# Batch 1 and the end in an order written out by hand, and the last value products between gates and in halves

## The chip, the cores and the metric

The kernel runs on one core of a Trainium2 chip. The metric is the device time of one execution in microseconds. Three runs of the kernel before took 674.27, 677.1 and 676.51 us; their median is 676.51.

## What is computed

Eight batches of tokens, 512 local and 32 global ones in each, with 8 heads of 64. Local tokens attend to the global ones and to a window of 32 to each side, global tokens to all; the result is x, with 512 channels. On x stands a feed-forward layer:

```python
x_prev = np.concatenate([np.zeros((B, 1, D)), x[:, :-1, :]], axis=1)
xk = mu_k * x + (1.0 - mu_k) * x_prev
xr = mu_r * x + (1.0 - mu_r) * x_prev
k = np.maximum(xk @ w_k, 0.0)
v = k * k @ w_v
r = 1.0 / (1.0 + np.exp(-(xr @ w_r)))
return (r * v).astype(np.float32)
```

Here w_k is 512x1024, w_v 1024x512 and w_r 512x512, all in f32.

## The kernel before

**Products.** The values are too fine for one pass of TensorE, so each operand is split into a high part (_h) and the rest (_l), and each product is three matmuls: high by high, high by rest, rest by high. The feed-forward layer works on 256 tokens at a time (a *half* of a batch, t0 and t1), the global tokens of all batches are one more set of 256 at the end. A *step* of it is 24 matmuls of 128x128 by 128x256. A half has four steps of keys (K), two of gates (G), and four of values.

**From batch 2 on** (`FROM = 2`) the values k*k @ w_v are made with seven products of blocks in place of eight: the left sides are blocks A11, A21, A12, A22 of w_v and sums S1 to S4 of them, the right sides blocks B11 to B22 of the squared keys and differences T1 to T4. The first three products are `values_1`, the other four `values_2`; `part` makes the two parts of a right side (a cast bh on DVE, the rest bl on DVE or POOL), `left_over` does this for those needed later. The left sides lie in DRAM (`scratch`) and are read back as `a<-scratch`. They are written in batch 1 by `sums_of_values`: for each of four i, two additions on POOL (L279), four more additions and subtractions on POOL (L284 to L287), a cast hs on ACT (L289), the rest ls on DVE (L290), and two stores on SP (L292).

**Mixing** of x with its predecessor (xk, xr) is DVE work with one subtraction on POOL for each of four pieces: k0, k2, r0, r2 (`mixing`, L603 to L613). The older `mix` does all four at once (L572 to L581).

**Attention** of the next pair of heads lies between the steps. For a pair, the steps called A are: four of transposes (four matmuls L144 each into the transpose bank ps_t, then a copy PT on ACT, L408), two of transposes for the global tokens, the second with the next scores, and one of weighted sums. Ahead of the transposes come a softmax on DVE and ACT (L362, L368), its reciprocal sums (L326, L327) and a multiplication on POOL (L374, and L447 for the global tokens).

**What sets the order.** TensorE's order is a chain of dependences in the order in which the program issues its matmuls. For ACT, DVE and POOL a scheduler picks the order, except between `by_hand.enter_context(tc.manual_schedule(...))` and `by_hand.close()`, where instructions stand on their engine in the order in which the code issues them. That stretch is batches 2 to 7. In it `in_turn` takes steps of attention (A) and feed-forward (F) by a string such as "AFAFAFAFAF", and the tables `todo` issue a piece of DVE or POOL work behind a step of a given number. Batch 1 is ordered by the scheduler: `together` spreads A and F evenly and `feed_forward` runs the halves. The end (the global tokens, `end()`) is too, since `by_hand.close()` stands ahead of it.

**PSUM.** ps_t has two banks in batch 1 (`SECOND_USE`) and one in the middle (`MIDDLE_USE`), with three banks ps_m for products; the end has seven of those.

In the text, steps of a batch are numbered from 0: F7 is the eighth feed-forward step, A9 the tenth step of attention.

Of the kernel before, what the change touches and what calls it, by code (L numbers as in the profile page):

```python
# [10 lines left out]
F32 = mybir.dt.float32  # L11
# [9 lines left out]
P = 128  # L21
# [45 lines left out]
def local_global_attention_then_rwkv_ffn(  # L67
# [12 lines left out]
    nc = tc.nc  # L80
# [186 lines left out]
    def sums_of_values():  # L267

        for i in range(HC):
            a = stage.tile([P, 2, 2, TOK], F32, tag="w64", name="a")  # L270
            hs, ls = (stage.tile([P, 4, TOK], F32R, tag="w64", name=f"{x}s") for x in "hl")
            for j in range(2):
                f = i + j * HC
                for x, part in enumerate((wv_h, wv_l)):
                    part = part[:, f].bitcast(F32).rearrange("p (e n) -> p e n", e=2)
                    store = nc.sync.dma_start(out=scratch[:, 2 * j:2 * j + 2, i, x], in_=part)
                    behind(store)
                with tc.issue_after(Tokens.square.ins):
                    nc.gpsimd.tensor_add(  # L279
                        a[:, j], *(w[:, f].bitcast(F32).rearrange("p (e n) -> p e n", e=2) for w in (wv_h, wv_l))  # L280
                    )
            a11, a21, a12, a22 = (a[:, j, e] for j in range(2) for e in range(2))

            nc.gpsimd.tensor_add(a22, a21, a22)  # L284
            nc.gpsimd.tensor_sub(a21, a11, a21)
            nc.gpsimd.tensor_sub(a11, a22, a11)
            nc.gpsimd.tensor_sub(a12, a12, a11)  # L287
            s = a.rearrange("p j e n -> p (j e) n")
            nc.scalar.copy(hs, s)  # L289
            nc.vector.tensor_sub(ls, s, hs.bitcast(F32))  # L290
# [258 lines left out]
    class Tokens:  # L549
# [114 lines left out]
        def values(self):  # L664
            for e0 in range(0, NC, 2):
# [8 lines left out]
                self.store(slice(e0, e0 + 2), o)  # L674
                yield

        def write(self, half, v):

            es = slice(2 * half, 2 * half + 2)
            o = self.gate[:, es]  # L680
            (nc.vector if v.tensor.name.startswith("ps_") else nc.gpsimd).tensor_mul(o, v, o)
            self.store(es, o)

    class Keys:
# [67 lines left out]
                    split(val, h, l, nc.vector if b[0] == "B" else nc.gpsimd)  # L752
                    self.parts[b].append((h, l))

        def product(self, out, b, fresh=True):
            right = self.parts.pop(b)
            for i in range(HC):
                a, (b_h, b_l) = left[i // 2], right[i // 2]
                for j in range(2):
                    a_h, a_l = (a[:, i % 2, x, j * P:(j + 1) * P] for x in range(2))  # L760
                    for n, (w, x) in enumerate(((a_h, b_h), (a_h, b_l), (a_l, b_h))):
                        matmul(
                            out[:, j], w, x[:, i % 2], start=fresh and (i, j, n) == (0, 0, 0),
                            stop=(i, n) == (HC - 1, 2), skip_group_check=True,
                        )
            del left[:HC // 2]
            load_left()

# [47 lines left out]
        def values_of_one(self):  # L816

            t, = self.tokens
            banks = self.bank(), self.bank()
            for b in range(2):  # L820
                parts = self.parts[f"B{b + 1}1"]
                for e, out in enumerate(banks):
                    self.parts[f"B{b + 1}1"] = parts
                    self.product(out, f"B{b + 1}1", fresh=not b)
                    if b:
                        t.write(e, out)
                    yield


    FF_STEPS = 6  # L830
    V_STEPS = 7

    def local_tokens(b, half, xT):
        at = half * TOK
# [11 lines left out]
    def feed_forward(tokens, before):  # L846

        for t in tokens:
            t.mix()
            if before is not None:  # L850
                yield from before.values()
            yield from t.keys_and_gate()
            before = feed_forward.last = t

    PAIR_STEPS = 8

# [187 lines left out]
    beside_heads(rest_of_first(), 2 * FF_STEPS + 2)  # L1044
    line["on"] = True
    leftp = sump = gate3 = None

    def batch(b, before):

        nonlocal leftp, sump, gate3  # L1050
        if b < FROM:
            sums = sums_of_values() if b == FROM - 1 else iter(())
            for n, _ in enumerate(feed_forward(tokens_of(b), before)):
                if n > FF_STEPS and n % 2:
                    next(sums, None)
                yield
            for _ in sums:
                pass
            return
        this = keys_at(b)  # L1060
        t0, t1 = this.tokens
# [15 lines left out]
                t.mixing(x)  # L1077

        def mix_next(*parts):
            if b + 1 < B:  # L1080
                mix(keys_at(b + 1).tokens[0], *parts)

        if b == FROM:
            t0.mix()
            steps = chain(before.values(), this.keys(t0), gates_of(0), this.keys(t1), gates_of(1))
            todo = {
                3: lambda: begin_halves(),
                7: lambda: mix(t1, "k0"),
                8: lambda: (mix(t1, "k2"), this.part("B11", 0)),
# [36 lines left out]
    early_u = valueu  # L1126
    by_hand = ExitStack()
    keys_of = {}

    def keys_at(b):  # L1130
        if b not in keys_of:
# [1 line left out]
        return keys_of[b]  # L1133

    BATCH = {
        FROM: "AFAFAFAFAF" "AFFAF" "AFAFAFAFAF" "AFFAF",
        None: "AFAFAFAFAF" "AFFAFF" "AFAFAFAFAF" "AFFFAFF",
    }
    last = first[1]
    for b in range(1, B):  # L1140
        if b == FROM:
            change_use(MIDDLE_USE)
            line["all"] = True
            by_hand.enter_context(tc.manual_schedule(engines={
                mybir.EngineType.Activation, mybir.EngineType.DVE, mybir.EngineType.Pool,
            }))
        if b < FROM:
            beside_heads(batch(b, last), 2 * FF_STEPS + 8)
            last = feed_forward.last
        elif b < B - 1:  # L1150
# [4 lines left out]
            last = keys_at(b)  # L1155
    final = Keys([global_tokens()])
    t, = final.tokens
    for _ in batch(B - 1, last):
        pass
    last = keys_of[B - 1]  # L1160
    by_hand.close()

    def end():
        t.mix()
# [6 lines left out]
        keys, gates, values = final.keys(t), t.gates(), last.values_2()  # L1171
        n = 5
# [12 lines left out]
    early_u.close()  # L1185


# [45 lines left out]
```

## Time and profile before

| | us |
|---|---|
| median of three runs | 676.51 |
| the profiled execution | 677.94 |
| its span, first to last instruction | 676.2 |
| PE idle between 206 and 216 us, in batch 1 | 5.9 |
| PE idle at the end of values_1 in the end | 2.8 |
| PE idle in the last two products, for a<-scratch | 1.7 |

The profile was taken on another execution than the three runs. Its page lists the busy time of every engine over the span (PE is TensorE's matmuls, PEld its weight loads, DVE VectorE, ACT ScalarE, POOL GpSimd, SP the engine that issues DMAs), the clock that TensorE was granted in 40 slices (9 is full speed), and the chain of work that ended last. Beside the page, the trace gives the waits of an engine with what ended them, the rows of an engine in order of time, and the busy time in any stretch.

### The profile page before, as it was taken

Reading aid. Unit: us, or ns where it says so; the run is one execution under the profiler, and the core shown is the slowest. Engines: PE = TensorE matmul, PEld = TensorE weight load, DVE = VectorE, ACT = ScalarE, POOL = GpSimd, SP = SyncE. Lnnn points to the kernel's source line nnn. Section 1 sums busy time; section 2 is a strip of 40 time slices with the busy share of each in tenths; the row PEclk is TensorE's granted clock in tenths of the full one; section 3 lists DMA queues with packets and bytes.
Section 4 is the critical chain, followed back from the end, with each engine's and each line's share of the span. In section 5 each row is a group of like instructions: output and inputs, shape, how many; then the busy total and the mean of one; then the engine's idle time right before and its main releaser. Section 6 shows DMA issues by size and latency. Waiting matters only on the chain.

```text
span 676.2 us, 20513 instructions
## 1 busy us (share of the span) xinstructions
PE 638.2 (94%) x8362; PEld 605.0 (89%) x8362; DVE 487.4 (72%) x1283; ACT 343.7 (51%) x1070; POOL 358.5 (53%) x326
## 2 busy tenths in 40 slices
PE   6779899999996899999999999999999999999896
PEld 3558789999985899989999999999999999999896
DVE  4687987617468339886989787986898678788531
ACT  4877786537273265737274637364746432313140
POOL 6376776425887124484448453755366435544720
PEclk9789999999998989999999999999999999999899
DMA  8826434514946550645846484727482653282455
GB/s 337 329 95 235 170 127 166 192 46 157 364 139 243 182 191 2 234 157 189 295 180 210 173 272 145 267 109 255 151 295 82 228 179 119 87 291 78 173 181 197
DMA packets 43549, 127.15 MB, mean 188 GB/s; under 512 B 4032, under 2 KB 20928, under 8 KB 43456
## 3 DMA queue, kind: packets, MB, share of 16 engines
q1 hardware_dynamic: 43456, 125.85, 53.0%
q8 instruction: 66, 1.08, 0.6%
q14 instruction: 27, 0.22, 0.1%
HBM read 108.53 MB, written 17.30 MB: 186 GB/s over the span
## 4 chain that ended last, share of the span: by engine, by line
PE 68%; DVE 7%; POOL 5%; ACT 2%; issue 2%; DMA 1%; POOLq 0%; DVEq 0%; ACTq 0%
PE ps_m L141 53%; PE ps_s L141 10%; PE ps_t L144 4%; DVE xfull L576 2%; ACT Pt L368 1%; DVE kkl L629 1%; DMA a<-scratch 1%; POOL Pt L374 1%; POOL a L279 1%; POOL xkl L581 1%; DVE Pt L362 1%; POOL k L625 1%; DVE diff L608 1%; DVE B L715 1%; POOL xrl L581 1%
## 5 line engine op out<-in xcount | busy, mean ns | idle before, releaser
L141 PE MATMUL ps_m<-xkh,wk_h 128*128 128x256 f32 x544 | 156.6, 288 | 4.5 <-DVE sum L785 2.8
L141 PE MATMUL ps_m<-xkh,wk_l 128*128 128x256 f32 x544 | 152.3, 280 | 1.8 <-issue 1.8
L141 PE MATMUL ps_m<-xkl,wk_h 128*128 128x256 f32 x544 | 153.0, 281 | 1.0 <-POOL xkl L581 1.0
L141 PE MATMUL ps_m<-bh,a 128*128 128x256 f32 x736 | 136.6, 282 | 1.7 <-DMA a<-scratch 1.7
L141 PEld LDWEIGHTS ps_m<-bh,a 128*128 128x128 f32 x736 | 114.7, 189 | 2.1 <-DMA a<-scratch 1.5
L374 POOL TENSOR_TENSOR Pt<-Pt,ssum 128x512 f32<-128x512 f32 x64 | 70.8, 1116 | 84.6 <-DVE ssum L327 63.6
L141 PEld LDWEIGHTS ps_m<-xkh,wk_h 128*128 128x128 f32 x544 | 103.7, 191 | 10.1 <-DVE sum L785 3.0
L368 ACT ACTIVATE Pt<-Pt,m 128x128 f32<-128x128 f32 x256 | 99.4, 393 | 14.8 <-DVE m L362 14.3
L141 PEld LDWEIGHTS ps_m<-xkh,wk_l 128*128 128x128 f32 x544 | 104.3, 192 | 2.0 <-issue 2.0
L141 PEld LDWEIGHTS ps_m<-xkl,wk_h 128*128 128x128 f32 x544 | 103.9, 191 | 2.0 <-POOL xkl L581 1.2
L141 PE MATMUL ps_m<-bl,a 128*128 128x256 f32 x368 | 102.7, 279 | 0.2 <-POOL bl L723 0.2
L644 ACT ACTIVATE relu<-ps_m 128x512 f32<-128x512 f32 x52 | 31.0, 596 | 95.2 <-PE ps_m L141 93.6
L141 PE MATMUL ps_m<-xrh,wr_h 128*128 128x256 f32 x272 | 77.1, 283 | 0.5 <-ACT relu L623 0.5
L141 PE MATMUL ps_m<-xrl,wr_h 128*128 128x256 f32 x272 | 75.5, 278 | 0.0
L141 PE MATMUL ps_m<-xrh,wr_l 128*128 128x256 f32 x272 | 75.3, 278 | 0.0
L362 DVE CUSTOM_DVE_ANT_0 Pt<-ps_s,masks 128x128 f32<-128x128 f32 x256 | 56.0, 285 | 20.0 <-PE ps_s L141 20.0
L141 PEld LDWEIGHTS ps_m<-bl,a 128*128 128x128 f32 x368 | 69.2, 188 | 0.4 <-POOL bl L723 0.4
L408 ACT COPY PT<-ps_t 128x512 f32<-128x512 f32 x56 | 32.6, 584 | 67.4 <-PE ps_t L144 67.4
L141 PE MATMUL ps_s<-raw_qk 64*32 64x128 f32 (+1 forms) x2112 | 56.7, 291 | 5.5 <-DMA raw_qk<-qk 5.4
L613 POOL TENSOR_TENSOR xkl<-xfull,xkh 128x512 fp32r<-128x512 f32 x22 | 29.6, 1345 | 57.7 <-DVE ssum L326 34.8
L723 POOL TENSOR_TENSOR bl<-B,bh 128x512 fp32r<-128x512 f32 x36 | 51.2, 1439 | 14.9 <-DVE bh L722 14.9
L722 DVE CAST bh<-B 128x512 fp32r<-128x512 f32 x72 | 49.5, 705 | 10.3 <-PE ps_m L141 10.3
(130 smaller groups left out, 1525.8 us busy)
## 6 DMA issues: line engine op xcount, KB each, us to landing
a<-scratch SPq DMA_DIRECT2D x92, 512.0 KB, 4.8
raw_v<-v SPq DMA_DIRECT2D x32, 896.0 KB, 7.3
raw_qk<-qk SPq DMA_DIRECT2D x32, 624.0 KB, 5.2
out_l<-gate SPq DMA_DIRECT2D x32, 256.0 KB, 4.3
w<-w_k SPq DMA_DIRECT2D x8, 512.0 KB, 9.5
w<-w_v SPq DMA_DIRECT2D x8, 512.0 KB, 3.5
w<-w_r SPq DMA_DIRECT2D x4, 512.0 KB, 3.8
scratch<-wv_h SPq DMA_DIRECT2D x8, 256.0 KB, 6.7
```

The costliest lines, as they stand in the source:

```text
L141: return in_line(nc.tensor.matmul(*a, **kw))
L144: return in_line(nc.tensor.transpose(*a, **kw))
L362: read = nc.vector.tensor_tensor_reduce(out=Pt[:, i], in0=place(t, n, h), in1=masks[:, 2 * slots[t][1] + n], op0=ALU.add, op1=ALU.min, sca ...
L368: nc.scalar.activation(Pt[:, i], Pt[:, i], AF.Exp, bias=low_x[:, i:i + 1], scale=-1.0, accum_out=ssum[:, i:i + 1],)
L374: nc.gpsimd.tensor_mul(Pt[:, some], Pt[:, some], inv.unsqueeze(2).to_broadcast([P, 4, W]))
L408: copy(pitched(j, h, 0, 4), tp.rearrange("p (g q) -> p g q", g=4))
L576: nc.vector.scalar_tensor_tensor(self.shape(xf[:, j]), self.shape(diff[:, j]), mu[:, c0 + j:c0 + j + 1], self.prev(c0 + j), op0=ALU.mult, ...
L581: nc.gpsimd.tensor_sub(lo[:, both], xf, hi[:, both].bitcast(F32))
L613: nc.gpsimd.tensor_sub(lo[:, both], xf, hi[:, both].bitcast(F32))
L644: nc.scalar.activation(rk, kp, AF.Relu)
L722: nc.vector.tensor_copy(h, val)
L723: (nc.vector if b[0] == "B" else nc.gpsimd).tensor_sub(l, val, h.bitcast(F32))
```

## The change

Batch 1 is put under the same regime as the others: the manual schedule and the middle use of the banks begin ahead of batch 1, and it has a string and a table of its own.

```diff
     BATCH = {
+        FROM - 1: "AFAFAFAFAF" "AFFAFFF" "AFAFAFAFAF" "AFFAFFF",
         FROM: "AFAFAFAFAF" "AFFAF" "AFAFAFAFAF" "AFFAF",
...
+    SUMS_AT = range(4, 20)
...
         if b < FROM:
-            sums = sums_of_values() if b == FROM - 1 else iter(())
-            for n, _ in enumerate(feed_forward(tokens_of(b), before)):
-                if n > FF_STEPS and n % 2:
+            t0, t1 = tokens = tokens_of(b)
+            steps = chain(before.values(), t0.keys_and_gate(), t0.values(), t1.keys_and_gate())
+            sums = sums_of_values()
+            todo = {
+                0: lambda: t0.mixing("k2"),
+                1: lambda: t0.mixing("r0"),
+                2: lambda: t0.mixing("r2"),
+                8: lambda: t1.mixing("k0"),
+                9: lambda: t1.mixing("k2"),
+                10: lambda: t1.mixing("r0"),
+                11: lambda: t1.mixing("r2"),
+                18: lambda: keys_at(FROM).tokens[0].mixing("k0"),
+                19: lambda: keys_at(FROM).tokens[0].mixing("k2"),
+            }
+            t0.mixing("k0")
+            for n, _ in enumerate(steps):
+                todo.get(n, lambda: None)()
+                if n in SUMS_AT:
                     next(sums, None)
                 yield
```

The sums of w_v are issued in quarters behind the steps F4 to F19: the first addition, the second, then L283 to L285, then L287 with the cast hs, ls and the stores. Their additions no longer wait for a square of the keys (`issue_after` is gone):

```diff
-                with tc.issue_after(Tokens.square.ins):
-                    nc.gpsimd.tensor_add(
-                        a[:, j], *(w[:, f].bitcast(F32).rearrange("p (e n) -> p e n", e=2) for w in (wv_h, wv_l))
-                    )
+                nc.gpsimd.tensor_add(
+                    a[:, j], *(w[:, f].bitcast(F32).rearrange("p (e n) -> p e n", e=2) for w in (wv_h, wv_l))
+                )
+                yield
...
             nc.gpsimd.tensor_add(a22, a21, a22)
             nc.gpsimd.tensor_sub(a21, a11, a21)
             nc.gpsimd.tensor_sub(a11, a22, a11)
+            yield
             nc.gpsimd.tensor_sub(a12, a12, a11)
             s = a.rearrange("p j e n -> p (j e) n")
             nc.scalar.copy(hs, s)
```

For ACT this gives the following order behind the gates of F8 and F9 in batch 1 (gate_2699), where the four copies PT are those of the transposes A7 to A10 and hs_2737 is the cast of i=1:

```order
L659 ACTIVATE gate_2699<-ps_m_2746 128x512
L661 ACTIVATE gate_2699<-gate_2699 128x1024
L408 COPY PT_206<-ps_t_2793 128x4x128
L408 COPY PT_206<-ps_t_2833 128x4x128
L289 CAST hs_2737<-a_2736 128x1024
L408 COPY PT_206<-ps_t_2874 128x4x128
L408 COPY PT_206<-ps_t_2911 128x4x128
```

Before, the cast of that i stood behind all four copies, and it was the cast of i=0 that stood among them (the gates are the first half's there as well):

```order
L659 ACTIVATE gate_2614<-ps_m_2729 128x512
L408 COPY PT_206<-ps_t_2779 128x4x128
L661 ACTIVATE gate_2614<-gate_2614 128x1024
L289 CAST hs_2598<-a_2597 128x1024
L408 COPY PT_206<-ps_t_2883 128x4x128
L408 COPY PT_206<-ps_t_2914 128x4x128
L408 COPY PT_206<-ps_t_2963 128x4x128
```

A cast stands among the copies in both orders; it is a different i, and the transposes now share one bank. The cast of i=3 stands ahead of the copies of batch 2's first pair in both kernels. On POOL the cast of i=1 stands behind these rows, from the end of i=0 (L374 and L447 are the softmax of the next pair, L613 the mixing of t1, L278 to L287 the sums):

```order
L374 TENSOR_TENSOR Pt<-Pt,ssum 128x512
L613 TENSOR_TENSOR xkl<-xfull,xkh 128x512
L278 TENSOR_TENSOR a<-wv_h,wv_l 128x512
L374 TENSOR_TENSOR Pt<-Pt,ssum 128x512
L613 TENSOR_TENSOR xkl<-xfull,xkh 128x512
L278 TENSOR_TENSOR a<-wv_h,wv_l 128x512
L447 TENSOR_SCALAR Pg<-Pg,ssumg 128x544
L613 TENSOR_TENSOR xrl<-diff,xrh 128x512
L283 TENSOR_TENSOR a<-a 128x256
L284 TENSOR_TENSOR a<-a 128x256
L285 TENSOR_TENSOR a<-a 128x256
L613 TENSOR_TENSOR xrl<-diff,xrh 128x512
```

The next row there is L287, which the cast reads. What moved are the pieces of mixing, which now stand between the additions of one i.

In batch 2 the first half is mixed in pieces: k0 and k2 behind F18 and F19 of batch 1, r0 and r2 behind its own F0 and F1. At the end, the global tokens (`final`) are mixed in batch 7 behind its steps F16 to F18, the last piece behind the first step of the end:

```diff
         def mix_next(*parts):
-            if b + 1 < B:
-                mix(keys_at(b + 1).tokens[0], *parts)
+            mix((keys_at(b + 1) if b + 1 < B else final).tokens[0], *parts)
...
     def end():
-        t.mix()
         for n, _ in enumerate(last.values_1()):
             last.left_over(n)
+            if n == 0:
+                t.mixing("r2")
             yield
```

The order of steps in the end changes as well. Before it was K K V K K V G V G V and then the products of `values_of_one` (E), with the parts of the global tokens' keys by `split` ahead of the E. Now E stands between the gates, and the parts come by `part`:

```diff
-        for stream in (keys, keys, values, keys, keys, values, gates, values, gates, values):
-            next(stream)
-            if stream is values and n < 7:
-                last.left_over(n)
-                n += 1
-            yield
-        for stream in (keys, gates, values):
-            yield from stream
-        final.split("B11", "B21")
-        yield from final.values_of_one()
+        keys, gates, values, ends = final.keys(t), t.gates(), last.values_2(), final.values_of_one()
+        todo = {
+            1: lambda: last.left_over(5),
+            3: lambda: last.left_over(6),
+            4: lambda: final.part("B11", 0),
+            5: lambda: (final.part("B11", 1), final.part("B21", 0)),
+            7: lambda: final.part("B21", 1),
+        }
+        for n, x in enumerate("KVKVKVKVEGEGEE"):
+            next({"K": keys, "V": values, "E": ends, "G": gates}[x], None)
+            todo.get(n, lambda: None)()
+            yield
...
+    by_hand.close()
```

`values_of_one` makes the global tokens' values in two outputs X and Y, each from two products. The last product, of Y, runs its first 128 channels to their end and then the others, each in a bank of its own, so that the first are multiplied by the gate and stored while the others run:

```diff
-        def product(self, out, b, fresh=True):
+        def product(self, out, b, fresh=True, apart=False, between=None):
...
+            steps = [(i, j) for i in range(HC) for j in range(2)]
+            if between:
+                steps.sort(key=lambda x: x[1])
...
+            product(X, 0)
+            yield
+            product(Y, 0, apart=True)
+            yield
+            product(X, 1)
+            t.write(0, X)
+            yield
+            product(Y, 1, apart=True, between=lambda j: t.write_one(2 + j, Y[j]))
+            yield
```

DVE's last rows before (bl are parts of the global tokens' keys, L681 multiplies the gate with a product's 128x512):

```order
L240 TENSOR_TENSOR bl_10109<-B21_9794,bh_10108 128x512
L240 TENSOR_TENSOR bl_10113<-B21_9794,bh_10112 128x512
L812 TENSOR_TENSOR sum_9701<-ps_m_9947,sum_9701 128x512
L681 TENSOR_TENSOR gate_9983<-ps_m_10116,gate_9983 128x512
L681 TENSOR_TENSOR gate_9983<-ps_m_10117,gate_9983 128x512
```

and now (L687 is the former L681, L680 is in `write_one`):

```order
L823 TENSOR_TENSOR sum_9696<-ps_m_9890,sum_9696 128x512
L728 CAST bh_10057<-B21_9793 128x512
L729 TENSOR_TENSOR bl_10058<-B21_9793,bh_10057 128x512
L687 TENSOR_TENSOR gate_10092<-ps_m_10061,gate_10092 128x512
L680 TENSOR_TENSOR gate_10092<-ps_m_10062,gate_10092 128x256
L680 TENSOR_TENSOR gate_10092<-ps_m_10063,gate_10092 128x256
```

The last multiplication is half as large, and a store stands on SP behind each of the two. The number of matmuls is the same in both kernels.

More of the change, by code (lines that the diff above doesn't have):

```diff
@@ L675, in values, with write_one @@
                 yield
+        def write_one(self, e, v):
+            o = self.gate[:, e]
+            nc.vector.tensor_mul(o, v, o)
+            self.store(slice(e, e + 1), self.gate[:, e:e + 1])
         def write(self, half, v):
@@ L753, in split @@
                     self.parts[b].append((h, l))
-        def product(self, out, b, fresh=True):
+        def product(self, out, b, fresh=True, apart=False, between=None):
             right = self.parts.pop(b)
-            for i in range(HC):
+            steps = [(i, j) for i in range(HC) for j in range(2)]
+            if between:
+                steps.sort(key=lambda x: x[1])
+            for i, j in steps:
                 a, (b_h, b_l) = left[i // 2], right[i // 2]
[L759 to L765, printed above, removed]
+                a_h, a_l = (a[:, i % 2, x, j * P:(j + 1) * P] for x in range(2))
+                for n, (w, x) in enumerate(((a_h, b_h), (a_h, b_l), (a_l, b_h))):
+                    matmul(
+                        out[j] if apart else out[:, j], w, x[:, i % 2],
+                        start=fresh and (i, n) == (0, 0) and (apart or j == 0),
+                        stop=(i, n) == (HC - 1, 2), skip_group_check=True,
+                    )
+                if between and i == HC - 1:
+                    between(j)
             del left[:HC // 2]
@@ L818, in values_of_one, with product @@
             t, = self.tokens
[L819 to L826, printed above, removed]
-                    yield
+            X, Y = self.bank(), [self.bank()[:, 0] for _ in range(2)]
+            parts = [self.parts[f"B{b}1"] for b in (1, 2)]
+            def product(out, b, **how):
+                self.parts["end"] = parts[b]
+                self.product(out, "end", fresh=not b, **how)
+            product(X, 0)
[7 more added lines that the diff above has]
+            yield
     FF_STEPS = 6
-    V_STEPS = 7
     def local_tokens(b, half, xT):
@@ L844, in global_tokens @@
                       lambda a: a.rearrange("p (b n) -> p b n", b=GB), store)
-    def feed_forward(tokens, before):
-        for t in tokens:
-            t.mix()
[L850 to L853, printed above, removed]
     PAIR_STEPS = 8
@@ L1058, in batch @@
                 pass
+            batch.last = t1
             return
@@ L1079, in mix_next @@
         def mix_next(*parts):
-            if b + 1 < B:
-                mix(keys_at(b + 1).tokens[0], *parts)
+            mix((keys_at(b + 1) if b + 1 < B else final).tokens[0], *parts)
         if b == FROM:
-            t0.mix()
             steps = chain(before.values(), this.keys(t0), gates_of(0), this.keys(t1), gates_of(1))
             todo = {
+                0: lambda: mix(t0, "r0"),
+                1: lambda: mix(t0, "r2"),
                 3: lambda: begin_halves(),
@@ L1128, in local_global_attention_then_rwkv_ffn @@
     keys_of = {}
+    final = Keys([global_tokens()])
     def keys_at(b):
@@ L1139, in local_global_attention_then_rwkv_ffn @@
     last = first[1]
-    for b in range(1, B):
[L1141 to L1150, printed above, removed]
+    change_use(MIDDLE_USE)
+    line["all"] = True
+    by_hand.enter_context(tc.manual_schedule(engines={
+        mybir.EngineType.Activation, mybir.EngineType.DVE, mybir.EngineType.Pool,
+    }))
+    for b in range(1, B):
+        if b < B - 1:
             ff = batch(b, last)
@@ L1154, in local_global_attention_then_rwkv_ffn @@
                 pass
-            last = keys_at(b)
-    final = Keys([global_tokens()])
+            last = keys_at(b) if b >= FROM else batch.last
     t, = final.tokens
```

4 lines of the change are left out of this document (removed).

## The prediction

> **What bounds the kernel now.** I read the page first, then PE's waits, then its windows.
>
> ```profile
> PE 638.2 (94%) x8362; PEld 605.0 (89%) x8362; DVE 487.4 (72%) x1283; ACT 343.7 (51%) x1070; POOL 358.5 (53%) x326
> ...
> PEclk9789999999998989999999999999999999999899
> ...
> PE 68%; DVE 7%; POOL 5%; ACT 2%; issue 2%; DMA 1%; POOLq 0%; DVEq 0%; ACTq 0%
> ```
>
> PE is busy for 94% of the span, no other engine for more than 72%, and PE carries 68% of the chain that ended last. The change leaves the number of matmuls as it is, so it can only move what PE loses: idle time, and time at a lower granted clock. PE's waits say where the large pieces are:
>
> ```profile
> PE ps_t L144 <- POOL xrl L581: 5.9, 1, 5.9
> ...
> PE ps_m L141 <- DVE sum L785: 2.8, 1, 2.8
> PE ps_m L141 <- issue: 1.8, 1, 1.8
> PE ps_m L141 <- DMA a<-scratch: 1.7, 2, 1.3
> ...
> PE ps_m L141 <- POOL bl L723: 0.2, 1, 0.2
> ```
>
> Columns: total us, times, longest. The windows (length, then busy time and count of PE, PEld, DVE, ACT, POOL, then PEclk) place them:
>
> ```profile
> 130.00:140.00 10.00, 10.00 (x88) 10.00 (x87) 3.69 (x11) 2.07 (x5) 3.50 (x3) 1.00 0.66 262
> ...
> 170.00:180.00 10.00, 9.38 (x81) 9.15 (x81) 7.62 (x11) 2.61 (x4) 8.57 (x8) 1.00 1.03 373
> ...
> 200.00:210.00 10.00, 7.62 (x78) 6.86 (x74) 7.96 (x13) 4.93 (x21) 9.29 (x9) 1.00 1.01 390
> 210.00:220.00 10.00, 5.23 (x25) 5.26 (x26) 9.02 (x15) 3.56 (x5) 5.79 (x5) 0.67 0.33 115
> ...
> 214.77:220.10 5.33, 5.33 (x25) 5.33 (x26) 5.12 (x9) 1.40 (x2) 1.52 (x2) 0.50 0.54 190
> ...
> 237.40:240.60 3.20, 3.20 (x17) 3.20 (x17) 0.00 (x0) 2.73 (x10) 0.00 (x0) 0.50 0.01 5
> ...
> 300.00:620.00 320.00, 320.00 (x4180) 311.66 (x4179) 263.02 (x637) 157.37 (x480) 164.12 (x127) 1.00 0.54 187
> ...
> 629.81:633.20 3.39, 3.39 (x16) 3.39 (x17) 3.39 (x4) 0.00 (x0) 3.39 (x4) 0.51 0.20 82
> ```
>
> From 300 to 620 us PE is busy all the time at full clock: there is nothing to win in the batches that were already ordered by hand. What batch 1 loses is in three rows: 0.62 us in 170 to 180, and 2.38 + 4.77 = 7.15 us in 200 to 220. After that idle time PE runs for 5.33 us at a clock of 0.50, which costs half of it, 2.65. **Batch 1 loses 10.4 us.** The matmul at 130 to 140 gives the unit for what follows: 10.00 us / 88 = 0.114 us each, so 2.73 us for one step of 24. After the end's wait of 2.8 us the clock is 0.51 for 3.39 us: 1.7 lost.
>
> The waits row names xrl, which is one row too late. ACT and POOL at that place:
>
> ```profile
> 212.60 1.04 ACT L289 CAST hs<-a 128x1024 fp32r<-128x1024 f32 x1 [5.86 <-POOL a L287]
> ...
> 214.04 0.58 ACT L408 COPY PT<-ps_t 128x512 f32<-128x512 f32 x1
> ...
> 211.67 0.90 POOL L287 TENSOR_TENSOR a<-a 128x256 f32<-128x256 f32 x1
> ```
>
> PE's next transposes need the only transpose bank, which the copy at 214.04 frees. That copy stands on ACT behind the cast hs, and the cast waited 5.86 us for POOL's last subtraction L287. **The mechanism of the stall is the hs cast ahead of the PT copies in ACT's queue.** So the question for the change is where it puts that cast.
>
> **The change in batch 1.** The 10.4 us go if the new order has no such place. The order has two. The cast of i=1 stands between the copies of the transposes A8 and A9, and that of i=3 ahead of batch 2's first copy. The price is worked out from POOL's durations:
>
> ```profile
> L374 POOL TENSOR_TENSOR Pt<-Pt,ssum 128x512 f32<-128x512 f32 x14 | 16.1, 1169 | 15.5 <-DVE ssum L327 14.1 <-ACT relu L623 1.5
> L625 POOL TENSOR_TENSOR k<-relu 128x512 f32<-128x512 f32 x10 | 11.1, 1112 | 13.3 <-ACT relu L623 13.1
> L279 POOL TENSOR_TENSOR a<-wv_h,wv_l 128x512 f32<-128x512 f32 x8 | 10.9, 1388 | 1.4 <-DVE ls L290 1.4
> ...
> L447 POOL TENSOR_SCALAR Pg<-Pg,ssumg 128x544 f32<-128x544 f32 x4 | 4.0, 1001 | 5.0 <-DVE ssumg L327 5.0
> L286 POOL TENSOR_TENSOR a<-a 128x256 f32<-128x256 f32 x4 | 3.5, 884 | 0.3
> L285 POOL TENSOR_TENSOR a<-a 128x256 f32<-128x256 f32 x4 | 3.3, 815 | 0.2
> L287 POOL TENSOR_TENSOR a<-a 128x256 f32<-128x256 f32 x4 | 3.1, 777 | 0.2
> L284 POOL TENSOR_TENSOR a<-a 128x256 f32<-128x256 f32 x4 | 3.0, 752 | 0.2
> ...
> L613 POOL TENSOR_TENSOR xkl<-xfull,xkh 128x512 fp32r<-128x512 f32 x14 | 18.1, 1291 | 29.1 <-DVE ssum L326 29.1
> L613 POOL TENSOR_TENSOR xrl<-diff,xrh 128x512 fp32r<-128x512 f32 x13 | 17.7, 1359 | 25.2 <-PE ps_t L144 14.2 <-DVE xrh L612 9.4 <-DMA a<-scratch 1.6
> ...
> L368 ACT ACTIVATE Pt<-Pt,m 128x128 f32<-128x128 f32 x256 | 99.4, 393 | 14.8 <-DVE m L362 14.3
> ```
>
> and from batch 2, which has the same softmax and mixing in by-hand order, but no sums of weights:
>
> ```profile
> 249.39 0.60 ACT L644 ACTIVATE relu<-ps_m 128x512 f32<-128x512 f32 x1 [1.18 <-PE ps_m L141]
> ...
> 253.96 1.41 POOL L613 TENSOR_TENSOR xkl<-xfull,xkh 128x512 fp32r<-128x512 f32 x1 [1.61 <-DVE xkh L612]
> ...
> 262.23 1.66 POOL L613 TENSOR_TENSOR xrl<-diff,xrh 128x512 fp32r<-128x512 f32 x1 [0.36 <-DVE xrh L612]
> ```
>
> *First stall.* Count from the start of the relu of step F7. PE needs the copy of A9 when it comes to A10. Ahead of that stand F8 to F12, five steps of 24, and three sets of four transposes: 132 matmuls x 0.114 = 15.0 us. On the other side: relu 0.6, L625 1.1, L287 0.8, the hs cast of i=0 1.0, four L368 of 0.39, and about 0.3 for DVE's reciprocal sums, 5.4. Then POOL does, in its queue's order, two L374 (2.34), two xkl (2.58), two weight additions (2.78), L447 (1.0), two xrl (2.72), L283 to L285 (2.45) and L287 (0.78): 14.65. One wait for an xkh as at 253.96 adds 1.6. L287 ends at 21.65, the cast at 22.7, the copy at 23.3: **a stall of 8.3 us**. From below: batch 2's last xrl ends 14.5 us after its relu began (263.89 - 249.39); were all added POOL work to fit in the idle time of that stretch, then L287, the cast and the copy would still end at 16.9, a stall of 1.9. From above: the slower xkl and xrl beside a busy DVE and two more waits for xrh of a microsecond each, 10.8. I take 8.3, since POOL's rows leave it little idle time there once the sums are in.
>
> *Second stall.* Count from F17's relu. PE reaches A1 of batch 2 after F18, F19, four transposes and F0: 76 x 0.114 = 8.6. POOL: relu 0.6, then L625, one addition, L374, xkl, L283 to L285, L374, xkl, L287: 1.11 + 1.39 + 1.17 + 1.29 + 2.45 + 1.17 + 1.29 + 0.78 = 10.65. With one wait of 1.6, 12.9; cast and copy to 14.5: **5.9 us**, between 4.3 (no wait) and 8 (a second wait, longer operations).
>
> *Clock.* PE's idle time cost 1.6 to 2.65 us more in the rows with 0.50; I take 2.1 for each of the two stalls. Batch 1 then loses 8.3 + 5.9 + 4.2 = 18.4 in place of 10.4: **+8.0**, between -1.0 (1.9 + 4.3 + 2 x 1.6 = 9.4) and +13.7 (10.8 + 8 + 2 x 2.65 = 24.1).
>
> The rest of that part I cost at nothing. Mixing in four pieces is the same DVE and POOL work, in steps in which the values of earlier tokens keep PE fed. The middle banks (one transpose bank, three m) are what batches 2 to 6 have, and those show no idle PE. The hs and ls stores on SP now stand ahead of loads for heads that come a whole pair later; if that cover fails, it shows as a wait for raw_qk or raw_v. The issue gap of 1.8 us, and the 1.6 of clock behind it (the row at 237.40), come in batch 2 behind work that stays; I leave both in.
>
> **The change at the end.**
>
> ```profile
> 619.71 0.41 DVE L572 TENSOR_TENSOR diff<-xg_all 128x256 f32<-128x256 f32 x1
> ...
> 625.58 2.91 DVE L576 SCALAR_TENSOR_TENSOR xfull<-diff,mu_r_sb,xg_all 128x256 f32<-128x256 f32 x2
> ...
> 629.08 0.68 DVE L785 TENSOR_TENSOR sum<-ps_m,sum 128x512 f32<-128x512 f32 x1
> ...
> 667.81 0.69 DVE L681 TENSOR_TENSOR gate<-ps_m,gate 128x512 f32<-128x512 f32 x1 [8.11 <-PE ps_m L141]
> ...
> 669.03 0.39 PE L141 MATMUL ps_m<-bh,a 128*128 128x256 f32 x1 [1.26 <-DMA a<-scratch]
> ...
> a<-scratch SPq DMA_DIRECT2D x92, 512.0 KB, 4.8
> ```
>
> The sum L785, for which PE waits 2.8 us, stands on DVE behind the mixing of the global tokens (2.91 us of L576 alone just before it). With that mixing in batch 7's last steps, where PE's windows show it fed and DVE is 82% busy (263.02 of 320), the wait goes: -2.8, and its clock, -1.7. What is late next: the parts of T3. Before, two steps K stand between the halves and they came just in time (the bl row: 0.2 us of wait). Now one K stands there, so they are due 2.7 us sooner; from above the new wait is 2.9. DVE and POOL have less to do there by the mixing, so it can be nothing. I take 1.2. The last two products waited 1.7 for a<-scratch; now a gate step stands between each, 2.7 us more against 4.8 us from issue to landing, and the slot is free two products earlier: -1.7 (nothing, if the slot isn't). The last multiplication is 128x256 in place of 128x512: 0.41 for 0.69 by the row at 619.71, and half as much to store: together -0.5, an estimate. **The end: -2.8 - 1.7 - 1.7 - 0.5 + 1.2 = -5.5**, between -6.7 (no new wait) and -2.1 (2.9 of wait and 1.7 of clock).
>
> [...]
>
> **Sum.** +8.0 - 5.5 = +2.5 us on the profiled execution's own 677.94 (the span of 676.2 and 1.7 around it): 680.4. That execution lies 1.4 above the median of the three, 676.51; from the median the forecast is 679.0. About 0.5% (3.4 us) is what a measurement of this kernel can tell from no change: faster is below 673.1, slower above 679.9.
>
> **Rivals.**
> - *POOL has the room* (0.22). The sums fall into POOL's idle time, and the stalls come out at 1.9 and 4.3. For it: batch 2's stretch has idle POOL time ahead of three of its operations. Against it: the queue is in order, and the additions stand between operations that wait. -1.0 - 5.5 = -6.5: 670.0.
> - *The hs cast costs all that it can* (0.20), the slower side. ACT's queue holds the copy of A9 behind the cast until POOL's L287 is done. It decides as soon as L287 ends later than 13.4 us after F7's relu (15.0 less cast and copy); at 10.8 and 8 us +13.7 - 5.5 = +8.2: 684.7. For it: the old stall had this very chain.
> - *The end's wait only changes its name* (0.10): PE waits for T3's parts for 2.9 us and loses the clock again. +8.0 - 2.1 = +5.9: 682.4. Against it: less work on DVE there.
> - *The issue gap doesn't recur* (0.13): nothing in the profile names its cause, and a shift of some instructions may remove it: 679.0 - 1.8 - 1.6 = 675.6.
> - The forecast itself (0.35), spread over 676 to 682.
>
> Faster: the first rival and a little of the fourth, 0.23. Slower: the second, the third, and some of the forecast's upper part, 0.37. The rest, 0.40. The range reaches from just above the first rival's value to the second's, 670.5 to 684.5. Both signs hold much of the chance; the forecast's own range is 676 to 682.
>
> **What would show it.** Right: in batch 1 PE waits at L144 of 6 to 10 us with ACT's hs at its end, idle behind POOL a L287; another of 4 to 8 us at batch 2's second transposes; a PEclk of 0.5 behind each; no wait for the sum of L785's place (L796 now), none for a<-scratch in the last products, a short one for bl. Wrong: PE without idle time between 160 and 230 us, then the first sum falls; or PE waits in the end as long as before under another name; or PE waits for raw_qk or raw_v behind the stores on SP.

## The result and the profile after

| | median us | runs | ratio to before |
|---|---|---|---|
| before | 676.01 | 674.27 to 677.1 (4) | |
| changed | 687.18 | 684.15 to 687.46 (4) | 1.0158 (1.0121 to 1.0194) |
| before, other chip | 676.56 | 671.06 to 682.58 (17) | |
| changed, other chip (E6) | 683.83 | 678.19 to 689.63 (6) | 1.0101 (1.0035 to 1.0166) |

The change made the kernel slower, by 1.2 to 1.9% in the first measurement and by 0.4 to 1.7% in the second. The forecast was 679.0 with a range to 684.5: the first median lies outside it, that of the later measurement just inside, and both lie well above the forecast. The profiled execution took 687.01 us, its span is 685.2.

The page of the changed kernel, its busy row, the granted clock in 40 slices and the chain that ended last:

```profile
PE 643.4 (94%) x8362; PEld 609.8 (89%) x8362; DVE 502.7 (73%) x1296; ACT 342.6 (50%) x1066; POOL 354.0 (52%) x326
...
PEclk9977979999889899999999999999999999999999
...
PE 79%; DVE 8%; DMA 4%; POOL 3%; issue 3%; ACT 2%; SPq 0%; POOLq 0%; DVEq 0%
```

PE is as busy as before, 94%. The clock row has its low digits in the first six slices (100 us), as before but lower, and around 190 and 230 us. PE's waits (total us, times, longest):

```profile
PE ps_t L144 <- ACT PT L408: 17.5, 4, 9.5
...
PE ps_m L141 <- POOL bl L729: 2.1, 2, 1.3
...
PE ps_m L141 <- issue: 1.3, 1, 1.3
```

The wait for L785's sum and the waits for a<-scratch are gone. In place of one stall of 5.9 us there are two, of 9.5 and 7.2, and now the view names their releaser rightly: the copy PT on ACT. The first of them, row by row on ACT, POOL and PE (start, length, and in brackets the idle time ahead):

```profile
167.10 0.60 ACT L623 ACTIVATE relu<-ps_m 128x512 f32<-128x512 f32 x1 [1.17 <-PE ps_m L141]
...
190.01 1.05 ACT L289 CAST hs<-a 128x1024 fp32r<-128x1024 f32 x1 [13.17 <-POOL a L287]
190.96 0.58 ACT L408 COPY PT<-ps_t 128x512 f32<-128x512 f32 x1
...
172.30 1.07 POOL L374 TENSOR_TENSOR Pt<-Pt,ssum 128x512 f32<-128x512 f32 x1 [2.78 <-DVE ssum L327]
175.11 1.29 POOL L613 TENSOR_TENSOR xkl<-xfull,xkh 128x512 fp32r<-128x512 f32 x1 [1.75 <-DVE ssum L326]
...
180.22 1.29 POOL L613 TENSOR_TENSOR xkl<-xfull,xkh 128x512 fp32r<-128x512 f32 x1 [1.22 <-DVE ssumg L326]
...
184.22 1.27 POOL L613 TENSOR_TENSOR xrl<-diff,xrh 128x512 fp32r<-128x512 f32 x1 [0.43 <-DVE xrh L612]
...
189.25 0.72 POOL L287 TENSOR_TENSOR a<-a 128x256 f32<-128x256 f32 x1
...
191.68 1.09 PE L144 MATMUL ps_t<-ident,Pt 128*128 128x128 f32 x4 [9.46 <-ACT PT L408]
```

ACT does nothing for 13.17 us and holds a finished set of transposes behind the cast. The releaser to read is that of the cast, POOL's L287. The second stall has the same form:

```profile
214.95 0.60 ACT L623 ACTIVATE relu<-ps_m 128x512 f32<-128x512 f32 x1 [0.70 <-PE ps_m L141]
...
229.19 1.05 ACT L289 CAST hs<-a 128x1024 fp32r<-128x1024 f32 x1 [7.10 <-POOL a L287]
...
230.86 1.09 PE L144 MATMUL ps_t<-ident,Pt 128*128 128x128 f32 x4 [7.24 <-ACT PT L408]
```

Where the time went, from windows of 1 us: idle is the sum of what PE was not busy, clock the sum of its busy time times (1 - PEclk), in us; the last part of a microsecond is left out. E6, E9 and E11 are second and third profiles of the two kernels.

| | 0 to 100 | 100 to 310 | 310 to 600 | from 600 |
|---|---|---|---|---|
| before: idle, clock | 17.3, 6.3 | 11.9, 4.4 | 0.0, 0.0 | 8.6, 1.6 |
| before again (E9) | 16.3, 8.2 | 12.2, 4.0 | 1.1, 0.0 | 7.0, 1.7 |
| changed | 15.7, 15.3 | 20.3, 3.6 | 0.3, 0.0 | 5.3, 0.0 |
| changed again (E6) | 16.5, 9.2 | 21.3, 5.3 | 0.0, 0.0 | 5.0, 0.0 |
| changed again (E11) | 15.7, 11.8 | 20.7, 5.8 | 0.9, 0.0 | 5.4, 0.0 |

By the means of the rows the change costs 25.7 - 16.3 = 9.4 us between 100 and 310 us and gains 9.4 - 5.2 = 4.2 in the end. The third part, 28.1 - 24.1 = 4.0 us more in the first 100 us, lies in a stretch in which both programs have the same instructions in the same order on every engine.

These sums come to 9.2 us, but the profiled executions differ by 6.9 by their means, so they count more than the time that was lost. A count by matmuls adds up. PE's first 1734 matmuls are the same, in the same order, in every profile of the study, and so are its 2703rd to 8026th. Cut at the end of the 1734th and at the starts of the 3501st and the 7851st, the spans fall into these parts, in us:

| | first 1734 matmuls | to the 3501st | to the 7851st | to the end |
|---|---|---|---|---|
| before | 132.3 | 140.5 | 333.6 | 69.8 |
| before again (E9) | 134.0 | 140.3 | 335.4 | 68.7 |
| changed | 138.9 | 147.4 | 334.3 | 64.5 |
| changed again (E6) | 133.5 | 150.0 | 333.8 | 64.8 |
| changed again (E11) | 136.0 | 149.9 | 334.7 | 64.5 |

By the means the change costs 8.7 us in the second part, gains 0.2 in the third and 4.6 in the last, 3.9 in all behind the 1734th matmul. The first part, ahead of the changed code, is 3.0 us longer, and 6.6 in the first pair of profiles.

### The profile page after: what moved, and what is told of

It is laid out like the page before. It is cut to its first block, busy times and chain, and to the rows that moved or that the text cites. A ratio compares the mean times of both kernels' runs of the same rounds, so it can differ in the third digit from the quotient of the medians.

```text
span 685.2 us, 20545 instructions
## 1 busy us (share of the span) xinstructions
PE 643.4 (94%) x8362; PEld 609.8 (89%) x8362; DVE 502.7 (73%) x1296; ACT 342.6 (50%) x1066; POOL 354.0 (52%) x326
## 4 chain that ended last, share of the span: by engine, by line
PE 79%; DVE 8%; DMA 4%; POOL 3%; issue 3%; ACT 2%; SPq 0%; POOLq 0%; DVEq 0%
PE ps_m L141 59%; PE ps_s L141 14%; PE ps_t L144 5%; DMA w<-w_k 2%; DMA raw_v<-v 2%; DVE diff L608 2%; PE ps_t L141 1%; DVE xfull L608 1%; DVE diff L603 1%; DVE B L721 1%; DVE xkh L612 1%; DVE kkl L629 1%; DMA w<-w_r 0%; ACT Pt L368 0%; ACT hs L289 0%
## 5 line engine op out<-in xcount | busy, mean ns | idle before, releaser
L374 POOL TENSOR_TENSOR Pt<-Pt,ssum 128x512 f32<-128x512 f32 x64 | 69.9, 1099 | 87.1 <-DVE ssum L327 51.2
L368 ACT ACTIVATE Pt<-Pt,m 128x128 f32<-128x128 f32 x256 | 99.4, 392 | 13.6 <-DVE m L362 12.9
L613 POOL TENSOR_TENSOR xkl<-xfull,xkh 128x512 fp32r<-128x512 f32 x30 | 40.1, 1336 | 68.2 <-DVE ssum L326 38.5
L362 DVE CUSTOM_DVE_ANT_0 Pt<-ps_s,masks 128x128 f32<-128x128 f32 x256 | 55.9, 285 | 21.8 <-PE ps_s L141 21.5
L613 POOL TENSOR_TENSOR xrl<-diff,xrh 128x512 fp32r<-128x512 f32 x30 | 41.0, 1366 | 46.5 <-DVE xrh L612 28.1
L141 PE MATMUL ps_s<-raw_qk 64*32 64x128 f32 (+1 forms) x2112 | 58.3, 294 | 5.6 <-DMA raw_qk<-qk 5.5
L144 PE MATMUL ps_t<-ident,Pt 128*128 128x128 f32 x256 | 40.4, 285 | 21.5 <-ACT PT L408 17.5
```

The source lines that it names most:

```text
L141: return in_line(nc.tensor.matmul(*a, **kw))
L144: return in_line(nc.tensor.transpose(*a, **kw))
L362: read = nc.vector.tensor_tensor_reduce(out=Pt[:, i], in0=place(t, n, h), in1=masks[:, 2 * slots[t][1] + n], op0=ALU.add, op1=ALU.min, sca ...
L368: nc.scalar.activation(Pt[:, i], Pt[:, i], AF.Exp, bias=low_x[:, i:i + 1], scale=-1.0, accum_out=ssum[:, i:i + 1],)
L374: nc.gpsimd.tensor_mul(Pt[:, some], Pt[:, some], inv.unsqueeze(2).to_broadcast([P, 4, W]))
L613: nc.gpsimd.tensor_sub(lo[:, both], xf, hi[:, both].bitcast(F32))
```

## The experiments

**E1, the end alone.** The diff without its part on batch 1: batch 1 stays with the scheduler, and the global tokens' mixing, the order of steps, `part` and the halves are as changed.

```diff
-        FROM - 1: "AFAFAFAFAF" "AFFAFFF" "AFAFAFAFAF" "AFFAFFF",
...
+        if b == FROM:
+            change_use(MIDDLE_USE)
...
+        if b < FROM:
+            beside_heads(batch(b, last), 2 * FF_STEPS + 8)
+            last = feed_forward.last
```

> The end of the change alone; batch 1 is as before. My theory (the end gains what its waits lost: PE idle 5.3 against 8.6 us and no half clock, so 4.9 us by the two traces): about 671 us, 4 to 6 below before, with a wait of about 2 us for the parts of T3. Rival (the wait only changes its name once batch 1 does not arrive late): no gain, within 2 us of before. On the first 100 us, whose code is the same in all kernels: if the 9 us more of half clock that the changed kernel shows there is chance, this run shows some value between 6 and 15 us; if it belongs to the change in batch 1, it shows about 6 as before.

Measured: 670.77 us (10 runs), ratio 0.9939 (0.99 to 0.9979), beside a kernel before at 675.04. PE's waits in the end:

```profile
PE ps_m L141 <- POOL bl L729: 0.4, 1, 0.4
PE ps_m L141 <- DVE sum L801: 0.3, 1, 0.3
...
PE ps_m L141 <- DVE sum L796: 0.2, 1, 0.2
```

L796 is the former L785: its wait falls from 2.8 to 0.2 us with the mixing moved out of the way. The gain of 4.3 us is what my theory gave. The half clock of the first 100 us came to 3.1 us, less than in any other profile and below what either reading had expected.

**E2, batch 1 alone.** The diff without its part on the end.

```diff
-            mix((keys_at(b + 1) if b + 1 < B else final).tokens[0], *parts)
+            if b + 1 < B:
+                mix(keys_at(b + 1).tokens[0], *parts)
...
     last = keys_of[B - 1]
+    by_hand.close()
...
     def end():
+        t.mix()
```

> Batch 1 by hand alone; the end is as before. My theory (two stalls behind the hs casts, 9.5 and 7.2 us, in place of one of 5.9): PE loses 7.6 us more between 100 and 310 us, so 683 to 684 us if the first 100 us cost the same as before. Rival (the longer half clock of the first 100 us comes with this part of the change): 690 us or more, with 15 us of half clock before 100 us again.

Measured: 683.97 us (4 runs), ratio 1.0111 (1.0042 to 1.018), with 8.9 us of half clock before 100 us. The two stalls are there. What I had not forecast is the rest of its list:

```profile
PE ps_t L144 <- ACT PT L408: 17.5, 4, 9.5
...
PE ps_m L141 <- DMA a<-scratch: 0.2, 1, 0.2
```

The wait for L785's sum isn't there, although the end and its mixing are as before. The static order tells why. The first matmul of the end's first K, before the change and in E2, with the semaphore that it waits for:

```
4849 L141 MATMUL ps_m_9795<-xkh_9642,wk_h_217 128x256 [waits DVE_49]
4846 L141 MATMUL ps_m_9797<-xkh_9644,wk_h_217 128x256 [waits Activation_49]
```

It writes another bank. The banks ps2 are used in turn; batch 1 with the middle use takes another number of them, so the end starts on the bank that ACT's copy L780 frees, early, and not on that of DVE's L785. From the 7851st matmul to the end E2 takes 65.5 us, with the old code there, where the changed kernel takes 64.5 to 64.8 and the kernel before 68.7 to 69.8.

**E3, the casts later.** The changed kernel with hs, ls and their stores apart from L287, a step or more later (i=1 behind F14, i=3 behind F2 of batch 2).

```diff
             nc.gpsimd.tensor_sub(a12, a12, a11)
+            yield
             s = a.rearrange("p j e n -> p (j e) n")
...
-    SUMS_AT = range(4, 20)
+    SUMS_AT = {**dict.fromkeys((4, 5, 6, 7, 9, 10, 11, 15, 16, 17), 1), **dict.fromkeys((8, 14, 18, 19), 2)}
...
+                2: lambda: next(batch.sums),
```

> The changed kernel, but each hs cast with its ls and stores is issued a step or more after L287 (for i=1 behind F14, for i=3 behind F2 of batch 2), so that no copy PT that PE needs soon stands behind it; POOL does the same rows in nearly the same order. My theory (ACT's queue holds the copies): the waits of 9.5 and 7.2 us go to under 1.5 us each, with their half clock of 3 us: 15 to 18 us below the changed kernel, 669 to 672. Rival (POOL is too full there, and PE waits for the next thing that POOL makes late): PE waits at least 4 us in each place under another name, 680 or more.

Measured: 665.99 us (4 runs), ratio 0.9849 (0.9789 to 0.9909), below the 669 to 672 that I had expected. The stall of 9.5 us is gone altogether, that of 7.2 has become 4.2:

```profile
PE ps_t L144 <- ACT PT L409: 5.1, 3, 4.2
...
215.99 1.04 ACT L290 CAST hs<-a 128x1024 fp32r<-128x1024 f32 x1 [7.91 <-POOL a L287]
```

POOL does the same rows in nearly the same order, and PE doesn't wait for it under another name. So it is ACT's queue, not POOL's load. What is left, above the 1.5 us that I had expected, is again a cast ahead of a copy; that i=3 was not put late enough is tried in E7 and E10.

**E4, the cast on DVE.** Same place in the program, other queue.

```diff
-            nc.scalar.copy(hs, s)
+            nc.vector.tensor_copy(hs, s)
```

> The changed kernel, but the hs cast is done by DVE in the same place of the program, so it stands directly ahead of ls in DVE's queue and ACT's queue is free of it. My theory (the wait is for the queue that holds the cast): the copies PT are no longer late, but DVE's rows behind the cast are held until L287 ends, so PE waits 0 to 4 us at scores or at a ps_m bank in each place: 672 to 680. Rival (POOL's fullness alone): as in the changed kernel, 685 or more.

Measured: 666.34 us (4 runs), ratio 0.985 (0.9795 to 0.9905), better than I had expected. The waits:

```profile
PE ps_t L144 <- POOL Pg L447: 3.3, 2, 2.2
...
PE ps_s L141 <- DVE m L362: 1.4, 1, 1.4
PE ps_t L144 <- ACT PT L408: 0.8, 2, 0.6
```

The copies are no longer late. In each place a small wait is left, of 1.4 and 2.2 us. The longer one is for a row that now stands behind the cast in DVE's queue, the sums for L447:

```profile
222.44 0.69 DVE L289 CAST hs<-a 128x1024 fp32r<-128x1024 f32 x1 [2.09 <-POOL a L287]
...
224.32 0.15 DVE L326 TENSOR_SCALAR ssumg<-ssumg 128x1 f32<-128x1 f32 x1
...
224.83 1.11 POOL L447 TENSOR_SCALAR Pg<-Pg,ssumg 128x544 f32<-128x544 f32 x1 [2.42 <-DVE ssumg L327]
```

The wait of 1.4 us goes a longer way: POOL's next addition waited 2.13 us for DVE's ls behind the cast, POOL's L625 stood behind that addition, DVE waited 3.12 us for L625, and the scores' row L362 stood behind that. One changed word takes 16.7 us of waiting down to 3.6: what stands behind the cast in DVE's queue was needed later than what stood behind it in ACT's.

**E5, the banks of the end.** The kernel before with one edit:

```diff
-    LAST_USE = {"m": [ps2, ps2, psx, ps4, ps4, ps4, ps4]}
+    LAST_USE = {"m": [psx, ps2, ps2, ps4, ps4, ps4, ps4]}
```

> The kernel before with one edit: the end's list of banks begins with psx in place of ps2, so that its first step K writes the bank that ACT L780 frees, not the one that DVE L785 frees; the mixing of the global tokens stays where it was. Theory A (what makes PE wait for 2.8 us is which bank the first K gets, as the run of batch 1 alone suggests, where that wait was gone with the end unchanged): no wait for L785's sum, no half clock behind it, 3 to 5 us below before, 670 to 672 us. Theory B (my prediction's reading, that it is the mixing ahead of L785 on DVE): the wait moves to the next K or stays, total PE wait there above 2 us, time within 1.5 us of before.

Measured: 674.67 us (12 runs) beside 676.56, ratio 0.9971 (0.9935 to 1.0008). In the list of waits the sum L785 is gone, with no half clock behind it; a<-scratch is left:

```profile
PE ps_t L144 <- POOL xrl L581: 5.9, 1, 5.9
...
PE ps_m L141 <- DMA a<-scratch: 1.0, 3, 0.5
```

The trace bears theory A out: another bank is enough, with the mixing where it was. The median is only 1.9 us below, where 3 to 5 were expected, and the time does not settle the size, since the interval reaches from 4.4 us faster to no gain. Its one profile does: from the 7851st matmul to the end it takes 64.6 us, 4.6 less than the kernel before by its mean and as little as the changed kernel.

**E6, E9 and E11, both kernels again.** The changed kernel (E6, E11) and the one before (E9), with no edit.

> The changed kernel once more, unchanged, for the clock in the first 100 us. Theory C (the half clock there is chance and has nothing to do with the change; from 100 us on the change costs 3 us): the median comes out 2 to 7 us above before, 678 to 683, with some of its runs at a mean clock of 0.975 or more. Theory D (the changed kernel runs that stretch at half clock for longer as a rule): 686 to 688 again, every run at a clock of 0.970 or less.

> The kernel before once more, for a second profile of it. If the wait of 2.8 us for L785's sum is a matter of banks and order alone, it is there again, between 2.5 and 3.1 us, and the stall of 5.9 us in batch 1 too. If the half clock of the first 100 us is chance, its sum lies anywhere from 3 to 15 us and need not be the 6.3 of the first profile.

> The changed kernel a third time, for its profile: both stalls again, 9.5 and 7.2 us within 0.3, since they follow from the queues; the half clock in the first 100 us is a new draw (15.3 and about 9 us so far). If it is over 12 us here as well, the changed kernel draws high as a rule and chance alone becomes a poor reading.

E6 measured 683.83 us (6 runs), E9 one execution of 680.14, E11 one of 686.89. The stalls and the wait come back within 0.2 us: 9.4 and 9.5 us in the changed kernel, 5.9 and 2.6 in the one before. The rows of E6 and of E9:

```profile
PE ps_t L144 <- ACT PT L408: 17.5, 4, 9.4
...
PE ps_t L144 <- POOL xrl L581: 5.9, 1, 5.9
PE ps_m L141 <- DVE sum L785: 2.6, 1, 2.6
```

The first 100 us do not come back; the row of their window (PE busy and PEclk are the first and the sixth figure behind the length), for the kernel before, the changed one, and the two again in E9 and E11:

```profile
0.00:100.00 100.00, 82.67 (x1269) 66.54 (x1269) 77.09 (x261) 72.47 (x241) 64.62 (x94) 0.93 0.59 213
...
0.00:100.00 100.00, 84.29 (x1129) 67.84 (x1130) 72.06 (x233) 66.64 (x215) 60.88 (x91) 0.85 0.56 203
...
0.00:100.00 100.00, 83.67 (x1237) 67.35 (x1237) 76.97 (x258) 70.87 (x234) 63.12 (x93) 0.91 0.57 208
...
0.00:100.00 100.00, 84.34 (x1156) 68.05 (x1158) 74.92 (x249) 69.24 (x227) 61.78 (x92) 0.88 0.57 208
```

PE's busy time differs by less than 2 us, the clock by up to 0.08, which is 8 us; where the clock is lower, fewer of the matmuls fall into the window. The executions of one kernel follow their mean clock: in E6 from 678.19 us at 0.980 to 689.63 at 0.965. Theory D as it was put (every run at 0.970 or less) falls, since two of the six runs have 0.980. Theory C's 678 to 683 was a little low. That the start is chance alone isn't shown: E11's half clock in the first 100 us, 11.8 us, is just under the 12 above which its expectation called chance a poor reading, and what the other runs add stands under "What stays open" below.

**E7 and E10, the cast of i=3 a step later still.**

```diff
-                2: lambda: next(batch.sums),
-                3: lambda: begin_halves(),
+                3: lambda: (next(batch.sums), begin_halves()),
```

> The casts later, as before, and that of i=3 one step later still (behind F3 of batch 2, ahead of the first load of the left sides). In the first version PE waited 4.2 us for the copy behind that cast, with 1.7 us of half clock. By the queue theory a step more (2.7 us) leaves at most 1.5 us of wait, and 3 to 5 us come off: 661 to 664. If POOL's L287 is itself what is late, the wait moves on with the cast and the time stays at 666.

> The kernel with the casts later and that of i=3 behind F3, once more, since the profile of its first run fell on an execution that was disturbed. By the queue theory PE's wait for the copy behind that cast (4.2 us in the first version) is under 1.5 us, the wait for bl is 2.0 as in the changed kernel, and the time is 661 to 667.

E7's profiled run took 3508 us and is left out; why is not known. The other five took 663.12 to 668.2 us, with a median of 663.44, ratio 0.9855 (0.9802 to 0.9907). E10, the same kernel on another chip, took 660.89 us (4 runs) beside 675.1, ratio 0.9782 (0.9702 to 0.9862). Its waits, and its row for 100 to 310 us:

```profile
PE ps_m L141 <- POOL bl L730: 2.1, 2, 1.3
...
PE ps_t L144 <- ACT PT L409: 0.8, 2, 0.6
...
100.00:310.00 210.00, 206.06 (x2974) 197.45 (x2972) 149.80 (x430) 121.31 (x400) 117.53 (x102) 1.00 0.53 187
```

The wait for the copy is 0.8 us, as in the kernel before, and between 100 and 310 us PE is idle for 4.0 us and never at half clock. The queue's reading holds here too: the wait did not move on with the cast.

**E8, two steps K ahead of the first product.** E7 with:

```diff
-        for n, x in enumerate("KVKVKVKVEGEGEE"):
+        for n, x in enumerate("KKVKVKVVEGEGEE"):
```

The pieces that `todo` issues from `left_over` and `part` come a step later with it.

> As the kernel with the casts two steps later, and the end begins with two steps K ahead of the first product of values_2, as before the change, in place of one. If the wait of 2.0 us for the parts bl is the price of the one K that was taken from between, as the prediction had it, it falls under 0.5 us and the time by 1 to 2 us. If another resource sets it (DVE's queue of parts), the wait comes back at a later product and the time stays.

Measured: 660.73 us (6 runs) beside 676.56 on the same chip, ratio 0.9768 (0.9705 to 0.9831); E7's five runs there have a median of 663.44. The wait for bl:

```profile
PE ps_m L141 <- POOL bl L730: 0.4, 1, 0.4
```

The 1.7 us come off the wait as expected, and from the 7851st matmul to the end the profile takes 62.9 us, 1.7 less than E10's 64.5. The medians of E8 and E7 differ by 2.7 us, but their runs overlap (654.5 to 664.84 and 663.12 to 668.2), so the time alone doesn't show the gain. E8 is the fastest version of the study, some 2.3% below the kernel before, and it holds the whole of the change but for the place of the sums' casts and of one K.

## Why the prediction was wrong

1. *The mechanism of the stalls: right.* The page named xrl; the prediction read the hs cast ahead of the copies. For the changed kernel's two stalls E3 and E4 show it, by moving the cast in time and to another queue. For the old stall no run moved the cast alone, and it rests on the rows that the prediction shows.
2. *The first stall: right in place, too small.* PE's due time was 15.0 us after F7's relu; in the trace it is 191.68 - 9.46 - 167.10 = 15.1. POOL was to begin at 5.4 (172.30 - 167.10 = 5.2). L287 was to end at 21.65 and ended at 22.9 (189.97 - 167.10): POOL waited three times for DVE, for 1.75, 1.22 and 0.43, where the sum took one wait of 1.6. So 9.5 in place of 8.3: POOL's waits for DVE were the term that was too small.
3. *The second stall: the same fault.* 7.2 in place of 5.9; due at 8.7 (8.6 in the sum), L287 at 14.2 (12.9). Together the two are 2.5 us short. Both fell inside the bounds of 10.8 and 8.
4. *The clock behind the stalls: right.* 4.2 was taken; the two windows behind them give 3.12 x 0.43 + 4.94 x 0.45 = 3.6:

```profile
191.68:194.80 3.12, 3.12 (x17) 3.12 (x18) 0.63 (x1) 0.59 (x1) 2.41 (x2) 0.57 0.95 336
230.86:235.80 4.94, 4.94 (x25) 4.94 (x26) 2.32 (x6) 0.59 (x1) 2.38 (x2) 0.55 0.62 216
```

5. *Batch 1 as a whole*: +8.0 in the sum, 8.7 by the count of matmuls and 9.4 by the windows. The wait "issue" of batch 2 came back (1.3 to 2.2 us), as the forecast had it.
6. *The end*: -5.5 in the sum, -4.6 by the count of matmuls and -4.2 by the windows. The new wait for bl was 2.1, not 1.2; E8 shows that it is the price of the K that was taken from between. The waits for a<-scratch did go, but in the second profile of the kernel before they were only 0.6 in place of 1.7, so 1.7 was one execution's value. The smaller last product and store gained 0.8 and not 0.5: from the start of the last matmul to the end of the span it is 4.3 us in both profiles of the kernel before and 3.5 in the three of the changed one.
7. *Why the 2.8 us went: half the reason.* With batch 1 as it was, moving the mixing does it (E1). But the first part of the change does it by itself, through the banks (E2, E5). I looked at what DVE had in its queue and not at which bank PE was about to write. That the term came out near its forecast is luck in this part. The gains of the two parts don't add: E2 with the old end took 683.97 us and the whole change 683.83, each in its own session, and behind the 7851st matmul E2's end is longer by only 0.8 us. Most of what the end part would have won was won already.
8. *The step that failed most: the time ahead of the changed code was put at nothing.* The sum put +2.5 on one execution's own time, as if the rest cost the same in every execution and in both kernels, and the range was built of the stalls' bounds alone. Behind the 1734th matmul the change costs 3.9 us (5.2 by the windows), which puts the forecast at about 680 to 682, inside the range. Of the 9.0 us between the first two profiled spans, 6.6 lie in the first 1734 matmuls. What is longer there is the time at half clock: in the first 100 us it costs 6.3 and 8.2 us in the two profiles of the kernel before, 15.3, 9.2 and 11.8 in the three of the changed one, 3.1 to 14.6 in the other kernels of the study, and the twelve profiles take 128.4 us (at 3.1) to 138.9 (at 15.3) for those matmuls. Three runs between 674.27 and 677.1 looked like a spread of 3 us; the later 17 went from 671.06 to 682.58.

The side was one that the prediction held open, slower with 0.37. The rival that came nearest, the hs cast at its full price, did so in the number alone: its stalls of 10.8 and 8 us did not come, and the start made up the difference.

What stays open: why the changed kernel is slower in its start, and whether it is so as a rule. Its three values can be three high draws, but the other runs lean the other way. An estimate: take from each run's lost clock, (1 - mean clock) x span, what the profiles of its kernel lose behind the 1734th matmul (0.1 to 10.2 us). On average 10.2 us are left in the 38 runs of kernels with batch 1 by hand, and 6.6 in the 60 of kernels with batch 1 by the scheduler; single runs of either kind spread by about 4. From 78 to 96 us PEclk is 0.72 to 0.91 in five of the eight profiles of the first kind and 1.00 in all four of the second. So the change may have a price ahead of its own code, of about 3 us. No run changed the start by itself, and nothing here shows how code that comes later would do it.

## What to carry to other kernels

- In an order by hand, look at each instruction that waits for another engine's last step (here a cast) and ask what stands behind it in its own queue and when that is needed; issue the producer early and the consumer two or three steps later, or put the consumer in a queue whose next rows have time. Here the 16.7 us of waiting came down to 4.2 in E3 and to 3.6 in E4.
- A wait for a bank can depend on the rotation: that of 2.8 us for L785's sum went with a change far ahead that takes another number of banks (E2), and with another first bank alone (E5). So read which bank the waiting instruction writes before giving the wait to the work ahead of its releaser.
- Ask how far the parts of the program that are not touched vary from one execution to the next, and put that in the range: here the same 1734 matmuls took 128.4 to 138.9 us. A median of three runs close together says little of it.
- Compare two profiles from one matmul to the same matmul, where the order allows it, and not only between two times: the parts then add up to the spans.

## What was not expected of the hardware

The clock that PE is granted in the start does not repeat from one execution to the next. In the stretch whose instructions are the same, from 44 to 62 us and from 85 to 95, the kernel before and the changed one show (PEclk is the third figure from the end):

```profile
44.00:62.00 18.00, 16.42 (x199) 12.95 (x200) 13.31 (x39) 12.39 (x44) 13.52 (x11) 0.81 0.48 163
85.00:95.00 10.00, 10.00 (x175) 9.17 (x175) 9.24 (x29) 7.77 (x25) 7.42 (x6) 1.00 0.27 87
...
44.00:62.00 18.00, 18.00 (x170) 13.93 (x171) 13.23 (x39) 9.00 (x31) 12.26 (x10) 0.53 0.40 134
85.00:95.00 10.00, 10.00 (x66) 8.48 (x67) 8.95 (x22) 3.60 (x10) 5.71 (x5) 0.51 0.15 54
```

In the second execution PE is at half clock for 17 of the 18 us of the first window (PEclk 0.53), although the view has it busy for all 18.00. It varies from run to run of one kernel as well: in E6 the mean clock goes from 0.965 to 0.980. What sets it, no run shows. Nor is it a matter of the first matmuls alone: the half clock comes again between 20 and 96 us, in the changed kernel's profile from 23 to 28, from 44 to 62 and from 85 to 96. In the first 100 us it costs 3.1 to 15.3 us in the twelve profiles, up to 2.2% of a span of 685 us.
